# Linear-attention block: 1/std and softmax reciprocals by Ln and Exp on ScalarE, another order of the first loads, block diagonals on GpSimd

## The chip, the cores and the metric

The kernel runs on one core of a Trainium2 chip. A core has a matmul engine (TensorE, PE in the profile; its weight loads are PEld), a vector engine (VectorE, DVE), an activation engine (ScalarE, ACT), GpSimd (POOL) and SyncE (SP), which issues transfers. Each engine works through its own queue strictly in order and waits on semaphores of the others. Transfers are issued from the queues of SP and ACT. The metric is device microseconds (us) of one execution, median of several runs.

## The reference

One transformer block on x of 2048 rows by 640 columns, in bf16:

```python
h  = x + A(layernorm(x))          # linear attention, H = 32 heads of Dh = 20
h2 = h + B(layernorm(h))          # GeGLU, F = 1536
# A: q, k, v = x @ wqkv;  pq = q @ w_phi (per head), pk = k @ w_phi
phi_k = concat([softmax(pk), softmax(-pk)])      # phi_q likewise
kv = sum_s phi_k * v;  z = sum_s phi_k
o  = (phi_q @ kv) / (phi_q @ z + 1e-6);  A = o @ wo
# B: (gelu(x @ w_gate) * (x @ w_up)) @ w_down
# layernorm: (x - mean) / sqrt(var + 1e-5), no weights
```

## The kernel before

The 2048 rows are 16 tiles of 128 (t = 0 to 15), in four blocks b of four tiles. `NC` = 5 is the number of 128-row chunks of 640. The order of work is written out by hand (`manual_schedule`) for every engine: what a line issues goes to the end of its engine's queue. PSUM tiles for matmul results come from a rotating pool of four (three in the k loop) slots, `gtile`.

*Start (lines 160 to 384).* The first loads: x tile 0, tiles 2-3, W_v in three pieces, tiles 4-5, the transposed W_k (`WkT`) by a transposing DMA, tiles 8-11, `WqT`, tiles 12-15 on SP's queue; x tile 1, w_phi, tiles 6-7 on ACT's queue. Ten matmuls on zeros (`warm`) keep PE busy until x has come. For each of the first tiles: `ln_st` takes statistics on DVE (two `bn_stats` of 320 columns, one `bn_aggr`) and then 1/std on POOL (an add of eps and a `pow` of -0.5); `ln_ap` scales the tile on DVE (`ln_dve`); `ln_tp` transposes it on PE and copies it out of PSUM on ACT. `v_part` and `v_mm` are the v matmuls, `v_ev` their evacuation on ACT into one of six `vS` buffers (20 columns a head and a column of ones). w_phi is folded into W_k and W_q (`fold`): block diagonals `BD`, made on DVE at line 356 from w_phi and a mask, are multiplied with the transposed weights; the results are cast out of PSUM in turn by ACT and DVE.

*k loop (lines 388 to 421).* For each tile t: `k_tile` (k matmuls, and on ACT the exponentials E of +pk and -pk), `v_tile(t + 4)`, the layernorm of tile t+6 on ACT (`ln_act`, which also needs `mr`, the negated mean times 1/std, from POOL) and its transposing DMA, statistics of two later tiles, and `k_norm`: on DVE the sums over each head's 20 columns, 64 sums a tile (`sk`), and their reciprocals (`rs`); then v times the reciprocal (`vt`), the half of -pk on POOL and the half of +pk on DVE or POOL (`VP` lists the tiles for POOL; DVE's is put off to the next tile by `todo`). `kv_tile` multiplies E with vt into `kvp`, the sum over all tiles, four or five tiles later. At t = 15 four groups of q matmuls and their exponentials (`q_mm`, `q_exp`) are issued ahead of `k_norm(15)`; then come the k·v sums of tiles 10 to 15 and `kv_mask`.

*Attention and GeGLU (lines 610 to 665).* For each tile, stages `attn_a` (matmuls with kv), `attn_b`, `attn_b2`, `attn_b3` (the division, transposed by DMA), `attn_c` (matmuls with W_o, `po`), `attn_d`, `attn_d2` (residual sum, statistics, with a Square on ACT and small operations on POOL) and `attn_e` (layernorm on ACT, then a transposing DMA into the block's `LN2T`). `weave` puts them between units of matmul work: `gate_up` (one 128-row piece of gate and up for columns a0 to a1 of the block, then Gelu on ACT, product on DVE) and `down` (half the columns of one output tile). A stage with index i is issued ahead of unit i; stages with an index beyond the last unit are carried into the next weave, with the index counted from there:

```python
656  weave(gus(0, 0, 256) + downs(0, (0, 1)), ...)
659  weave(gus(0, 256, 512) + downs(0, (2, 3)), attn_at(7, 1, SHORT2))
SHORT2 = (0, 2, 3, 4, 10, 10, 11, 13)
```

The second weave has 12 gate units and 4 down units (0 to 15). The next one begins with `attn_a(8)` and the gate units of block 1, which read all four tiles of `LN2T`. Outputs are stored by SP a few units after their sums.

Of the kernel before, what the change touches and what calls it, by code (L numbers as in the profile page):

```python
# [17 lines left out]
def kernel(  # L18
# [16 lines left out]
    H = 32  # L35
# [11 lines left out]
    NWARM = 10  # L47
# [5 lines left out]
    WA, WB = 2,0  # L53
    T3 = 3
# [31 lines left out]
    nhalf = const.tile([P, 2], F32, name="nhalf")  # L86

# [11 lines left out]
    def ln_stats(pool, tiles, tag, act=True, between=None):  # L99
# [12 lines left out]
        nc.gpsimd.tensor_scalar_add(ve, mv[:, :, 1], EPS)  # L112
        rstd = small(pool, [P, n], "rstd" + tag)
        nc.gpsimd.tensor_tensor(rstd, ve, nhalf[:, 0:n], op=ALU.pow)  # L114
# [38 lines left out]
    vS = [p1.tile([P, H, VC], BF16, name=f"vS{i}") for i in range(6)]  # L153
# [6 lines left out]
    nc.gpsimd.memset(nhalf, -0.5)  # L160
    nc.sync.dma_start(x_sb[0][:, 0:1, :], x_v[:, 0:1, :])
    nc.scalar.dma_start(x_sb[0][:, 1:2, :], x_v[:, 1:2, :])
    nc.sync.dma_start(x_sb[0][:, 2:4, :], x_v[:, 2:4, :])
    for c0, c1 in ((0, 2), (2, 4), (4, 5)):
        nc.sync.dma_start(Wv[:, c0:c1, :], w_v[:, c0:c1, 2 * D:3 * D])

    ones = fp.tile([P, 2], F32, name="ones")
    nc.scalar.activation(ones, nhalf, ACTF.Exp)
    nc.scalar.dma_start(wphi, phi_v.rearrange("(c p) f -> p c f", p=P))
    nc.sync.dma_start(x_sb[1][:, 0:2, :], x_v[:, 4:6, :])  # L170
    nc.scalar.dma_start(x_sb[1][:, 2:4, :], x_v[:, 6:8, :])
    nc.sync.dma_start_transpose(WkT, A_wqkv[:, D:2 * D])
    wo_v = A_wo.rearrange("(c p) n -> p c n", p=P)
# [9 lines left out]
    for i in range(6):  # L183
        nc.vector.memset(vS[i][:, :, Dh], 1.0)
    make_identity(nc, ident)
    nc.gpsimd.memset(hmask, 1.0)
    for c in range(NC):
# [4 lines left out]
                                compare_op=ALU.is_ge, fill=0.0, base=Dh - 1 - off, channel_multiplier=-1)  # L192

# [36 lines left out]
    def ln_st(*tiles, act=True, between=None):  # L230
        for t, v in zip(tiles, ln_stats(p1, [x_sb[t // 4][:, t % 4, :] for t in tiles], "1", act, between)):
            lnp[t] = v
# [37 lines left out]
    def v_ev(t):  # L270
        nc.scalar.copy(vS[t % 6][:, :, 0:Dh].rearrange("p (u h) f -> p u h f", u=2),
                       pv[t][:, :, 0:HD].rearrange("p u (h f) -> p u h f", f=Dh))
# [5 lines left out]
    def k_tile(t):  # L278
# [3 lines left out]
        for s in range(2):  # L282
            nc.scalar.activation(Ek[t][:, s, :].rearrange("p (u f) -> p u f", u=2), pk[:, :, 0:HD],  # L283
                                 ACTF.Exp, scale=(1.0 if s == 0 else -1.0))

    def k_norm(t):


        sk = small(p1, [P, 2 * H], "sk")
        nc.vector.reduce_sum(sk, Ek[t].rearrange("p s (h f) -> p (s h) f", f=Dh), axis=AX.X)  # L290
        if t - 1 in todo:
            todo.pop(t - 1)()
        rs = small(p1, [P, 2 * H], "rs")
        nc.vector.reciprocal(rs, sk)  # L294
        Vt[t] = vt = ev.tile([P, 2, H, VC], BF16, name="vt", bufs=8)

        def mult(s, eng):
            eng.tensor_tensor(vt[:, s], vS[t % 6], rs[:, s * H:(s + 1) * H, None].to_broadcast([P, H, VC]), ALU.mult)  # L298

        mult(1, nc.gpsimd)  # L300
        if t in VP:
            mult(0, nc.gpsimd)
        elif t == NT - 1:
            mult(0, nc.vector)
        else:
            todo[t] = lambda: mult(0, nc.vector)

    todo = {}
# [36 lines left out]
    ln_st(0, act=False)  # L345
    ln_st(1, act=False)
    ln_ap(0, on_pe=True)
    ln_tp(0)
    warm(WA)
    ln_st(2, act=False, between=lambda: ln_ap(1, on_pe=True))  # L350
    ln_tp(1)
    warm(WB)
    ln_st(3, act=False)
    ln_ap(2, on_pe=True)

    nc.vector.tensor_tensor(BD, wphi[:, :, None, :].to_broadcast([P, NC, 8, Dh]),
# [340 lines left out]
```

The softmax here doesn't subtract the row's maximum and nothing guards it: scores larger than these inputs give would overflow.

## Time and profile before

| | |
|---|---|
| runs | 281.5, 281.89, 282.31 us; median 281.89 |
| the profiled execution | 281.18 us, of which the span from first to last instruction is 279.4 us |
| granted clock of TensorE | 1.00 |
| busy | PE 271.9, DVE 166.0, ACT 139.9, POOL 96.5 us |
| 1/std on POOL (line 114) | 8 of one column, mean 0.672 us; 5 of two columns, mean 0.713 us |
| reciprocals of k's sums (line 294) | 16, mean 0.547 us on DVE |
| k-loop layernorms on ACT (line 125) | 9, mean 0.933 us; on DVE (line 130) 9, mean 0.443 us |
| block diagonals (line 356) | 0.973 us on DVE |
| transposed W_k | issued at 4.52 us, 8.2 us from issue to landing |

How to read it: times in a chain or timeline are us from the start of the span, then the length. A chain is followed back from the last instruction to what released it at each step. "Idle before" is the time in which an engine had nothing running ahead of an instruction, and the arrow names what ended that. A busy PE includes its pipeline's latency, so neighbouring matmuls overlap in the timeline; the chain shows them end to end.

### The profile page before, as it was taken

What the parts mean: (1) busy time and instruction counts of PE and PEld (TensorE: products, weight loads), DVE (VectorE), ACT (ScalarE), POOL (GpSimd) and SP (SyncE); (2) the same over time, 40 slices, a digit from 0 to 9 for tenths busy, and PEclk for the clock granted to TensorE, in tenths of its full rate; (3) what the DMA queues carried; (4) which work ended last, traced back from release to release, by engine and by line L of the source; (5) the groups of instructions that cost most, each with busy time, mean ns of one, the idle gap of its engine ahead of it and who ended that gap; (6) DMA issues with size and microseconds to landing.
All of it is one profiled execution on the core that took longest, in us unless ns stands there. A gap on an engine that the chain in (4) does not pass through costs nothing.

```text
span 279.4 us, 5750 instructions
## 1 busy us (share of the span) xinstructions
PE 271.9 (97%) x2326; PEld 171.5 (61%) x2326; DVE 166.0 (59%) x289; ACT 139.9 (50%) x226; POOL 96.5 (35%) x211
## 2 busy tenths in 40 slices
PE   5899999999999999999999999999999999999995
PEld 2676677774655788788764555675455567444573
DVE  5899998789396586676324848322667532333222
ACT  2589888758596847355434454413446340222200
POOL 5448986794302216453401243300135230000000
PEclk9999999999999999999999999999999999999999
DMA  7991323694440021322520103221031513000011
GB/s 231 265 260 25 55 49 46 176 396 158 142 145 0 2 45 29 70 50 68 52 70 2 36 20 66 42 77 47 2 47 23 74 23 94 26 1 0 0 49 47
DMA packets 40347, 21.05 MB, mean 75 GB/s; under 512 B 33152, under 2 KB 38400, under 8 KB 40320
## 3 DMA queue, kind: packets, MB, share of 16 engines
q1 hardware_dynamic: 39376, 20.16, 28.8%
q10 hardware_dynamic: 944, 0.52, 0.7%
q8 instruction: 18, 0.29, 0.5%
q14 instruction: 9, 0.07, 0.1%
HBM read 10.18 MB, written 2.62 MB: 46 GB/s over the span
## 4 chain that ended last, share of the span: by engine, by line
PE 89%; DVE 4%; ACT 3%; DMA 1%; POOL 1%; issue 1%; ACTq 0%
PE gu L554 37%; PE pd L569 19%; PE pq L338 8%; PE po L509 8%; PE pk L251 7%; PE pv L251 5%; PE ab L449 2%; PE kvp L316 2%; DVE stats L106 1%; DMA x_sb<-in_A_x_dram 1%; DVE sk L290 1%; ACT E L283 1%; POOL rstd L114 1%; ACT Eq L343 1%; PE wa L215 1%
## 5 line engine op out<-in xcount | busy, mean ns | idle before, releaser
L557 ACT ACTIVATE g<-gu 128x512 bf16<-128x512 f32 (+1 forms) x60 | 30.7, 512 | 76.1 <-PE gu L554 75.1
L560 DVE TENSOR_TENSOR GT<-gu,g 128x512 bf16<-128x512 f32 (+1 forms) x60 | 34.5, 581 | 53.6 <-ACT g L557 53.4
L554 PE MATMUL gu<-LN2T,Wg 128*128 128x512 bf16 (+1 forms) x300 | 61.9, 337 | 0.5 <-DVE GT L560 0.4
L554 PE MATMUL gu<-LN2T,Wu 128*128 128x512 bf16 (+1 forms) x300 | 61.7, 336 | 0.0
L569 PE MATMUL pd<-Wd,GT 128*128 128x320 bf16 x384 | 53.8, 299 | 0.0
L569 PEld LDWEIGHTS <-GT 128*128 128x128 bf16 x384 | 37.4, 98 | 15.7 <-DVE GT L560 0.9
L554 PEld LDWEIGHTS <-Wu 128*128 128x128 bf16 x300 | 29.4, 98 | 22.6
L554 PEld LDWEIGHTS <-Wg 128*128 128x128 bf16 x300 | 28.4, 98 | 21.3 <-issue 0.5
L251 PEld LDWEIGHTS <-LN1T 128*128 128x128 bf16 x300 | 28.5, 98 | 11.6 <-issue 0.7
L298 POOL TENSOR_TENSOR vt<-vS,rs 128x672 bf16<-128x672 bf16 x22 | 29.2, 1345 | 9.1 <-DVE rs L294 8.5
L575 DVE TENSOR_TENSOR y<-pd,x_sb 128x640 bf16<-128x640 f32 (+1 forms) x17 | 13.3, 784 | 30.6 <-PE pd L569 30.6
L457 ACT COPY AB<-ab 128x704 f32<-128x704 f32 x28 | 19.5, 748 | 13.7 <-PE ab L449 13.5
L290 DVE TENSOR_REDUCE sk<-E 128x64 f32<-128x1280 bf16 x16 | 23.3, 1455 | 3.4 <-ACT E L283 3.4
L490 DVE TENSOR_TENSOR tt<-AB,w 128x1280 bf16<-128x1280 f32 x16 | 23.8, 1486 | 2.1 <-POOL w L483 2.0
L251 PE MATMUL pk<-Wk,LN1T 128*128 128x320 bf16 x160 | 24.1, 299 | 0.4 <-ACT E L283 0.3
L509 PE MATMUL po<-Wo,oT 128*128 128x320 bf16 x160 | 24.4, 299 | 0.0
L283 ACT ACTIVATE E<-pk 128x640 bf16<-128x640 f32 x32 | 20.8, 705 | 6.9 <-PE pk L251 6.7
L338 PE MATMUL pq<-LN1T,Wq 128*128 128x512 bf16 x100 | 22.9, 379 | 0.0
L251 PE MATMUL pv<-Wv,LN1T 128*128 128x320 bf16 x140 | 21.3, 299 | 0.0
L343 ACT ACTIVATE Eq<-pq 128x1024 bf16<-128x1024 f32 (+1 forms) x22 | 19.4, 950 | 3.7 <-PE pq L338 3.7
L509 PEld LDWEIGHTS <-oT 128*128 128x128 bf16 x160 | 15.6, 98 | 7.2 <-ACT oT L139 0.2
L125 ACT ACTIVATE ln<-x_sb,v,rstd 128x640 bf16<-128x640 bf16 x14 | 12.9, 919 | 10.5 <-POOL v L537 10.3
(80 smaller groups left out, 258.8 us busy)
## 6 DMA issues: line engine op xcount, KB each, us to landing
out_dram<-y SPq DMA_DIRECT2D x15, 160.0 KB, 1.8
Wg<-in_B_w_gate_dram SPq DMA_DIRECT2D x1, 1920.0 KB, 7.6
Wu<-in_B_w_up_dram SPq DMA_DIRECT2D x1, 1920.0 KB, 15.1
Wd<-in_B_w_down_dram SPq DMA_DIRECT2D x1, 1920.0 KB, 8.0
x_sb<-in_A_x_dram SPq DMA_DIRECT2D x2, 640.0 KB, 4.7
Wo<-in_A_wo_dram SPq DMA_DIRECT2D x1, 800.0 KB, 9.3
x_sb<-in_A_x_dram SPq DMA_DIRECT2D x2, 320.0 KB, 4.8
Wv<-in_A_wqkv_dram SPq DMA_DIRECT2D x2, 320.0 KB, 6.2
```

Of the source, the lines that this page charges most:

```text
L251: nc.tensor.matmul(ps[:, u, 0:HD], lhsT=lnT(t, c), rhs=W[:, c, u * HD:(u + 1) * HD], start=(c == 0), stop=(c == NC - 1))
L283: nc.scalar.activation(Ek[t][:, s, :].rearrange("p (u f) -> p u f", u=2), pk[:, :, 0:HD], ACTF.Exp, scale=(1.0 if s == 0 else -1.0))
L290: nc.vector.reduce_sum(sk, Ek[t].rearrange("p s (h f) -> p (s h) f", f=Dh), axis=AX.X)
L298: eng.tensor_tensor(vt[:, s], vS[t % 6], rs[:, s * H:(s + 1) * H, None].to_broadcast([P, H, VC]), ALU.mult)
L338: nc.tensor.matmul(pqs[j][:, i, :], lhsT=Wq2[:, kc, c * P:(c + 1) * P], rhs=LN1T[b][:, kc, :], start=(kc == 0), stop=(kc == NC - 1))
L343: nc.scalar.activation(Eq[j][:, :, s, :], pqs[j][:, 0:len(QG[j])], ACTF.Exp, scale=(1.0, -1.0)[s])
L490: nc.vector.tensor_tensor(tt.rearrange("p s (h f) -> p s h f", f=Dh), num, w[:, :, :, None].to_broadcast([P, 2, H, Dh]), ALU.mult)
L509: nc.tensor.matmul(po[:, u, 0:HD], lhsT=st[t][:, c, :], rhs=Wo[:, c, u * HD:(u + 1) * HD], start=(c == 0), stop=(c == NC - 1))
L554: nc.tensor.matmul(gu[:, i, 0:n], lhsT=W[:, c, f * P:(f + 1) * P], rhs=LN2T[b][:, c, a0:a1], start=(c == 0), stop=(c == NC - 1))
L557: nc.scalar.activation(g[:, 0:n], gu[:, 0, 0:n], ACTF.Gelu_apprx_tanh)
L560: nc.vector.tensor_tensor(st[b, "g", f][:, a0:a1], gu[:, 1, 0:n], g[:, 0:n], ALU.mult)
L569: nc.tensor.matmul(pd[:, u, 0:HD], lhsT=st[b, "g", f][:, tl * P:(tl + 1) * P], rhs=Wd[:, f, u * HD:(u + 1) * HD], start=(f == 0), stop=(f ...
```

## The change

- 1/std of tiles 0 to 3: `Ln(var + eps)` and `Exp(-0.5 ·)` on ACT (`log=True`) instead of POOL's add and pow; a table set that holds both functions is loaded at the top by hand.
- The reciprocals of k's sums: Ln and Exp on ACT (`k_rs`), for tile t-1 behind the exponentials of tile t; for tile 15 in `k_rs(15)` behind `k_norm(15)`. The sums are taken in two halves, and vt of tile t-1 follows the sums of tile t (`k_vt`).
- The layernorms of tiles 6 to 15 go from ACT (tile 6: DVE before too) to DVE, and POOL's `mr` with them.
- Block diagonals on POOL, right after the masks.
- Loads: x tile 1 on SP, tiles 2-3 on ACT ahead of w_phi, tiles 6-7 on SP behind the transposed W_k.
- The order of the first v matmuls, one warm-up matmul more at the top and one less later, 7 `vS` buffers, the pool's switch at tile 4 (`T3`) instead of 3.
- One Gelu on two columns ahead of the first real one; the last down unit in 192 and 128 columns; `attn_at(7, 3, SHORT2)` for `attn_at(7, 1, SHORT2)`.

```diff
-    NWARM = 10
+    NWARM = 11
-    WA, WB = 2,0
-    T3 = 3
+    WA = 1
+    T3 = 4
@@ ln_stats
-        nc.gpsimd.tensor_scalar_add(ve, mv[:, :, 1], EPS)
-        nc.gpsimd.tensor_tensor(rstd, ve, nhalf[:, 0:n], op=ALU.pow)
+        if log:
+            nc.scalar.activation(ve, mv[:, :, 1], ACTF.Ln, bias=eps)
+            nc.scalar.activation(rstd, ve, ACTF.Exp, scale=-0.5)
+        else:
+            nc.gpsimd.tensor_scalar_add(ve, mv[:, :, 1], EPS)
+            nc.gpsimd.tensor_tensor(rstd, ve, nhalf[:, 0:n], op=ALU.pow)
@@ loads
     nc.sync.dma_start(x_sb[0][:, 0:1, :], x_v[:, 0:1, :])
-    nc.scalar.dma_start(x_sb[0][:, 1:2, :], x_v[:, 1:2, :])
-    nc.sync.dma_start(x_sb[0][:, 2:4, :], x_v[:, 2:4, :])
-    for c0, c1 in ((0, 2), (2, 4), (4, 5)):
-        nc.sync.dma_start(Wv[:, c0:c1, :], w_v[:, c0:c1, 2 * D:3 * D])
-    ones = fp.tile([P, 2], F32, name="ones")
-    nc.scalar.activation(ones, nhalf, ACTF.Exp)
+    nc.sync.dma_start(x_sb[0][:, 1:2, :], x_v[:, 1:2, :])
+    nc.scalar.add_instruction(mybir.InstLoadActFuncSet(name=nc.get_next_instruction_name(), act_func_set_id=6))
+    nc.sync.dma_start(Wv[:, 0:2, :], w_v[:, 0:2, 2 * D:3 * D])
+    nc.scalar.dma_start(x_sb[0][:, 2:4, :], x_v[:, 2:4, :])
     nc.scalar.dma_start(wphi, phi_v.rearrange("(c p) f -> p c f", p=P))
+    nc.sync.dma_start(Wv[:, 2:4, :], w_v[:, 2:4, 2 * D:3 * D])
+    nc.sync.dma_start(Wv[:, 4:5, :], w_v[:, 4:5, 2 * D:3 * D])
     nc.sync.dma_start(x_sb[1][:, 0:2, :], x_v[:, 4:6, :])
-    nc.scalar.dma_start(x_sb[1][:, 2:4, :], x_v[:, 6:8, :])
     nc.sync.dma_start_transpose(WkT, A_wqkv[:, D:2 * D])
+    nc.sync.dma_start(x_sb[1][:, 2:4, :], x_v[:, 6:8, :])
@@ after the masks
+    nc.gpsimd.tensor_tensor(BD, wphi[:, :, None, :].to_broadcast([P, NC, 8, Dh]),
+                            hmask[:, :, :, None].to_broadcast([P, NC, 8, Dh]), ALU.mult)
@@ k_tile, behind the two exponentials
+        if t > 0:
+            k_rs(t - 1)
+    def k_rs(t):
+        sk = st1[t]
+        nc.scalar.activation(sk, sk, ACTF.Ln)
+        st1[t] = rs = small(p1, [P, 2 * H], "rs")
+        nc.scalar.activation(rs, sk, ACTF.Exp, scale=-1.0)
@@ k_norm
-        nc.vector.reduce_sum(sk, Ek[t].rearrange("p s (h f) -> p (s h) f", f=Dh), axis=AX.X)
-        if t - 1 in todo:
-            todo.pop(t - 1)()
-        rs = small(p1, [P, 2 * H], "rs")
-        nc.vector.reciprocal(rs, sk)
...
+        st1[t] = sk = small(p1, [P, 2 * H], "sk")
+        for s in range(2):
+            nc.vector.reduce_sum(sk[:, s * H:(s + 1) * H], Ek[t][:, s, :].rearrange("p (h f) -> p h f", f=Dh), axis=AX.X)
+    def k_vt(t):
+        rs = st1[t]
+        Vt[t] = vt = ev.tile([P, 2, H, VC], BF16, name="vt", bufs=8)
+        for s in (1, 0):
+            eng = nc.gpsimd if s == 1 or t in VP else nc.vector
+            eng.tensor_tensor(vt[:, s], vS[t % 7], rs[:, s * H:(s + 1) * H, None].to_broadcast([P, H, VC]), ALU.mult)
@@ start
-    ln_st(0, act=False)
-    ln_st(1, act=False)
-    ln_ap(0, on_pe=True)
+    ln_st(0, act=False, log=True)
+    ln_st(1, act=False, between=lambda: ln_ap(0, on_pe=True), log=True)
     ln_tp(0)
     warm(WA)
-    ln_st(2, act=False, between=lambda: ln_ap(1, on_pe=True))
+    v_part(0, 0, 1, 2)
+    ln_st(2, act=False, between=lambda: ln_ap(1, on_pe=True), log=True)
     ln_tp(1)
-    warm(WB)
-    ln_st(3, act=False)
-    ln_ap(2, on_pe=True)
-    nc.vector.tensor_tensor(BD, wphi[:, :, None, :].to_broadcast([P, NC, 8, Dh]),
-                            hmask[:, :, :, None].to_broadcast([P, NC, 8, Dh]), ALU.mult)
-    ln_ap(3, on_pe=True)
-    v_part(0, 0, 1, 2, 3, 4)
-    v_part(1, 0, 1)
-    ln_tp(2)
+    v_part(0, 3, 4)
+    v_part(1, 0, 1)
+    ln_st(3, act=False, between=lambda: ln_ap(2, on_pe=True), log=True)
+    ln_tp(2)
+    ln_ap(3, on_pe=True)
     v_part(1, 2, 3, 4)
     ln_tp(3)
@@ k loop
         if t > 0 and t + 6 < NT:
-            ln_ap(t + 6, on_act=True)
+            ln_ap(t + 6)
         if t % 2 == 0 and t + 8 < NT:
-            ln_st(t + 8, t + 9)
+            ln_st(t + 8, t + 9, act=False)
         k_norm(t)
+        if t > 0:
+            k_vt(t - 1)
+        if t == NT - 1:
+            k_rs(t)
+            k_vt(t)
@@ down, the last half tile
+        cuts = [(0, 192), (192, HD)] if last and u == 1 else [(0, HD)]
@@ behind q_exp(q + 6)
+    dummy = small(p2, [P, 2], "dummy", 1)
+    nc.scalar.activation(dummy, nhalf, ACTF.Gelu_apprx_tanh)
@@ second weave
-    weave(gus(0, 256, 512) + downs(0, (2, 3)), attn_at(7, 1, SHORT2))
+    weave(gus(0, 256, 512) + downs(0, (2, 3)), attn_at(7, 3, SHORT2))
```

## The prediction

> **What bounds the kernel now.** I read the page's busy shares first, then busy time by stretch, then the chain that ended last in order of time, then the timeline where the change touches something.
>
> ```profile
> PE 271.9 (97%) x2326; PEld 171.5 (61%) x2326; DVE 166.0 (59%) x289; ACT 139.9 (50%) x226; POOL 96.5 (35%) x211
> ```
> ```profile
> 0.00:16.86 16.86, 13.06 (x108) 8.21 (x109) 12.32 (x37) 7.98 (x13) 8.68 (x31) 1.00 0.98 256
> 16.86:31.61 14.75, 14.47 (x112) 10.28 (x111) 14.37 (x29) 12.47 (x20) 10.82 (x16) 1.00 0.36 90
> 31.61:72.49 40.88, 40.88 (x560) 28.36 (x560) 34.66 (x46) 32.55 (x47) 29.91 (x34) 1.00 0.49 146
> 144.14:276.46 132.32, 132.31 (x869) 73.28 (x868) 58.13 (x89) 45.10 (x76) 25.24 (x72) 1.00 0.16 36
> ```
> Columns: stretch, its length, busy us of PE, PEld, DVE, ACT, POOL, granted clock, DMA share, GB/s. From 31.61 on PE has work without a hole (but for 0.6 us near 95). So whatever makes DVE, ACT or POOL shorter there is worth nothing, and each wait that comes new to PE is paid in full. Something can be won only before 31.61, near 95 and behind the last matmul.
>
> ```profile
> 6.67 0.57 POOL rstd L114
> ...
> 9.74 1.42 POOL rstd L114
> ...
> 31.61 1.52 PE pk L251 x10
> ...
> 70.07 2.42 PE kvp L316 x120
> 72.49 2.27 PE pq L338 x10
> ...
> 134.67 1.36 PE po L509 x10
> 136.03 1.09 PE gu L554 x10
> 137.12 6.52 PE pd L569 x48
> 143.64 0.50 PE ab L449 x20
> 144.14 4.42 PE gu L554 x20
> ```
> Start, length, work. At the start the chain runs through POOL's 1/std; at 70 (the k·v sums) and at 144 (the second block's first gate matmuls) it is all PE. These two are where the change moves something to later:
>
> ```profile
> 69.03 2.92 ACT L343 ACTIVATE Eq<-pq 128x1024 bf16<-128x1024 f32 x4 [0.22 <-PE pq L338]
> 69.12 0.86 DVE L298 TENSOR_TENSOR vt<-vS,rs 128x672 bf16<-128x672 bf16 x1
> 69.19 1.97 POOL L298 TENSOR_TENSOR vt<-vS,rs 128x672 bf16<-128x672 bf16 x1 [1.34 <-DVE rs L294]
> ...
> 93.58 1.28 ACT L557 ACT_TABLE_LOAD   x1
> ```
> ```profile
> L298 POOL TENSOR_TENSOR vt<-vS,rs x22: 1309/1316/1969, 22.8 to 69.2; 128x672 bf16<-128x672 bf16 x22
> L298 DVE TENSOR_TENSOR vt<-vS,rs x10: 847/849/1009, 27.9 to 69.1; 128x672 bf16<-128x672 bf16 x10
> ```
> ```profile
> 137.44 0.73 ACT L530 ACTIVATE sq<-x_sb 128x640 bf16<-128x640 bf16 x1
> ...
> 139.75 0.92 ACT L125 ACTIVATE ln<-x_sb,v,rstd 128x640 bf16<-128x640 bf16 x1 [1.49 <-POOL v L537]
> ```
> ```profile
> DMA to landing us min/median/max: 2.5/2.6/4.5
> ```
> First fence: both halves of vt(15) are at work beside the last q exponentials, and end at 69.98 and 71.16, before PE needs them (72.09, see 3). The last two: tile 7's second layernorm, which lands (139.75+0.92+2.6) at 143.3, 0.9 us before the gate matmuls at 144.14.
>
> **The change, part by part.** Times are those of this execution's clock; who stands behind whom in a queue is read from the instruction order of the two built kernels.
>
> (1) *Start, to the fold of W_k (14.01 before).* Now: aggregate ends 5.09, POOL add and pow, scale at 6.10: 1.01 us. On ScalarE: Ln and Exp at 0.20 each (the 128x2 Exp at the top, 0.203) with 0.03 between: 0.5 us. So each scale could come 0.5 earlier, and the fourth, which waited for the 1.42 pow, 0.9. But the same engine copies the transposes out (0.69 each), in order: ahead of tile 0's copy now stands tile 1's Ln/Exp, which waits for tile 1's aggregate. Chain: statistics 3.96 to 5.09, Ln/Exp, scale 0 at 5.57; second half of tile 1's statistics and aggregate to 6.66; Ln/Exp to 7.11; copy 0 to 7.81, against 7.78 before. The gain is given back there. From copy 0 PE runs 6 v matmuls (0.82), transposes (0.28), 4 (0.54), waits for copy 1 to 9.86, 2 more weights of tile 1 (0.54), transposes, 0.82, 0.28, tile 2 (1.36) and half of 3 (0.68): fold at 13.82. Gain 0.2. Against it: x tiles 2-3 (320 KB) now go on ACT's queue beside tile 0 instead of behind it on SP's. Lower end 0, upper 0.9 (half of 4.8 less 3.1 us, the landings of 320 and 160 KB); I take 0.2, since SP's first packets lead. Tile 1 comes second on SP instead of first on ACT, near 4.5 instead of 4.1, and is wanted at 5.0: free. Sum of (1): 0, ends -0.4 (ACT's two at 0.15) and +0.7.
>
> What is nearly free here: block diagonals leave DVE (0.97) for POOL, (800/672)x1.345=1.6 us, ready by 8, needed at 14. The 11th warm-up matmul (0.43 at most) and the 7th buffer's memset (0.09) end before PE's first transposes and DVE's first x tile. The two-matmul warm-up becomes one, in time that PE waits anyway. There are two table loads before and after.
>
> But DVE and POOL get in each other's way: POOL's add took 0.41 beside the first scale (0.23 alone), and one DVE vt took 1.009 (0.849 alone) against a running POOL vt. So block diagonals that start ahead of a scale may hold it, by 0.16 (that row) or by their whole 1.6 us. At scale 1 this costs nothing: its transposes wait for PE's first 6 v matmuls until 8.66 anyway. At scale 0 it would count (rival A). The Trainium skill, SBUF — State Buffer, The single rule, speaks against the move more sharply than the rows: the two share one port pair, and whoever starts first holds it for its whole instruction. By that page a lost race costs the whole 1.6.
>
> W_k: its transposing DMA waits for x tile 0's landing (3.94) instead of tile 1's: issue 3.97, not 4.52; 6.11 us of issue on SP, to 10.1. Only then come x tiles 6-7 (before on ACT's queue at 1.72). They land 3.1 (160 KB) to 4.7 us (640 KB) later: 13.2 to 14.8; I take 13.4. DVE wants them at 13.0 (tiles 4 and 5's statistics, 4x0.41, behind scale 3); behind them stand DVE's W_k cast (14.6) and the scales of tiles 4 and 5, for which PE has about 0.4 us of slack, so 13.8 is early enough. Cost 0, upper end 1.0. x tiles 8-11 and W_q issue within 0.1 of before.
>
> Trainium skill, ScalarE: Activation LUTs, What ACT_TABLE_LOAD costs: an ACTIVATE with a per-partition bias is 0.28 us before its elements, not the row's 0.20; copy 0 would then come 0.3 later, and the sum below be 285.3.
>
> (2) *k loop, 16.9 to 62.5.* DVE: 16 reciprocals leave (8.8), 9 scales come (0.44 each, 4.0), the split sums cost some 0.1 more a tile (1.6): -3.2. POOL loses the small negated means (10 at 0.455). ACT: 9 scales leave (8.4), 32 Ln/Exp of 0.20+62x0.0008=0.25 come (8.2): even. The new wait: ACT's Ln of tile t-1 waits for DVE's sums; behind it queue v's evacuation and the next E. Adding DVE's rows in its new order (sums 1.5 a tile, a scale 0.4, a pair's statistics 1.9, vt 0.85, a W_q cast 0.75), sums 0 to 5 end near 21.8, 23.6, 27.2, 29.8, 33.4, 36.7, and ACT arrives after E of the next tile, near 22.5, 25.2, 28.0, 30.7, 33.7, 38.2: no wait. PE's holes of 0.08 at 26.7 (a transpose landing from ACT's late scale) and 0.28 at 31.3 (E of tile 4) close: -0.35; ends -0.4, +0.3.
>
> (3) *Last k tile.* Its Ln/Exp stand in ACT's queue behind the eight q exponentials, which end at 69.03+2.92=71.95, paced by PE's q matmuls. Then 2x0.25: 72.4. Both halves of vt(15) start there, DVE 0.86, POOL 1.97 as at 69.19, where the same two ran side by side: 73.3 and 74.4. PE has done tiles 10 to 14 at 70.07+100x0.0202=72.09 and has nothing else ahead of it; it ends the sums at 74.4+0.2=74.65 instead of 72.49. **+2.2**. Lower end with POOL's 1.32 alone: +1.5; upper 2.4. KV's masking shifts with it, covered by 2.27 of q as before.
>
> (4) *Dummy Gelu.* The table load already started 0.02 after the last Eq (93.58), with no wait in front; the dummy (0.20, less overlap) only stands ahead of the first g, which PE waits for near 95.4: +0.15; 0 to 0.2.
>
> (5) *Tile 7's start, 1 to 3.* Its attn_c goes from unit 11 to 13, its attn_e from 14 to 16, and the weave has units 0 to 15: it falls into the next one, though its order on PE shows one down unit (1.63) and one gate unit (1.09) now ahead of po: +2.72. po ends 138.75; statistics, square, POOL, ln and DMA took 7.2 from po's end (136.03) to 143.3, of which 0.5 was ACT busy with a g, absent now: landed 145.45. PE's next gate block needs all four tiles at 144.14: **+1.3**, ends 1.0 and 1.7. Cover: none, down units are done, attn_a(8) (0.50) is counted.
>
> (6) *Tail.* The last 320 columns split in 192 and 128: same matmul time; the last add is 0.29 instead of 0.49 (0.82 for 640, 0.49 for 320, so 1.03 ns a column): -0.2, ends -0.3, 0. The extra store issues (0.33) before the last one is ready.
>
> Sum: 0-0.35+2.2+0.15+1.3-0.2=+3.1. The profiled execution took 281.18, so 284.3; it lies 0.7 under the median 281.89, so **285.0**.
>
> **Rivals.** A: the block diagonals win the port before scale 0. w_phi landed 1.29+4.0=5.3 before, now behind 320 KB instead of 160: near 5.7, and scale 0 is due 5.6 to 5.8. For: a tie. Against: with scale 0 first, the block diagonals only meet scale 1. Price: scale 0 waits from 5.8 to 5.7+1.6-0.1=7.2, and the whole chain of (1) behind it, +1.4: 286.4. B: x tiles 6-7 late at 14.8: +1.0, 286.0. For: SP's 6.11 issue; against: 13.4 needs no help. C: one of the late stages is covered: without (3) 282.8, without (5) 283.7. For: an Eq run that ends earlier, or a quick landing; against: both orders are fixed. D, not slower: the four early 1/std really start PE 0.5 earlier and close all its holes up to 31.6 (0.46, 0.58, 0.31 and 0.36 beside its wait), 2.4 us at most; with the tail -0.2 and (3), (5) at their low ends (+2.5) that is 281.8. It decides from a gain of about 2.4 on; against it stands copy 0 at 7.81.
>
> **How the numbers follow.** Forecast 0.47 (own range 284.2 to 285.8), A 0.24, B 0.10, C 0.13, D 0.06. The range leaves out D and C's lower case, and takes in A with the upper ends of (3) and (5): 282.9 to 287.0. About 0.3% (0.85 us) is what a measurement can tell from no change. Faster 0.04 (most of D); same 0.05 (rest of D and C's lower case); slower 0.91.
>
> **What would show it.** PE idle of some 2 us between kvp matmuls, ended by POOL vt, just after the eighth Eq; PE idle of 1.3 before the first 512-wide gu, ended by DMA LN2T; fold of W_k within 0.4 of 14.0 (15.4 under A, with a first scale after 6.9); no wait of ACT on DVE sums. Wrong if kvp runs through, if LN2T lands before ab(8) ends, or if the k loop shows ACT waiting.

## The result and the profile after

The changed kernel took 292.96 us (median of 4 runs, 291.01 to 294.06) beside 281.83 us for the kernel before (281.50 to 282.31): 1.0386 times as long, 95% interval 1.0329 to 1.0443. The forecast of 285.0 us had the sign and missed the size; 292.96 lies outside its range of 282.9 to 287.0. The profiled execution took 293.0 us with a span of 291.3, against a span of 279.4 before: 11.9 us to be found.

The busy shares of the changed kernel, and its stretches from one event on TensorE to the next (columns as in the prediction):

```profile
PE 276.6 (95%) x2338; PEld 173.9 (60%) x2338; DVE 170.2 (58%) x299; ACT 140.4 (48%) x257; POOL 93.3 (32%) x195
```
```profile
0.00:16.47 16.47, 12.81 (x67) 6.94 (x68) 10.14 (x33) 6.97 (x16) 5.74 (x24) 0.90 0.99 255
19.32:68.71 49.39, 45.33 (x516) 33.15 (x515) 46.89 (x76) 34.59 (x73) 32.43 (x37) 1.00 0.41 121
68.71:81.29 12.58, 10.52 (x158) 5.91 (x156) 6.48 (x8) 9.34 (x17) 6.56 (x4) 1.00 0.14 55
81.29:102.94 21.65, 21.53 (x165) 11.03 (x166) 14.28 (x31) 14.46 (x18) 2.50 (x5) 0.92 0.28 92
156.13:288.57 132.44, 132.40 (x880) 73.83 (x880) 58.15 (x89) 43.74 (x75) 25.24 (x72) 1.00 0.17 37
```

The first row ends where the fold of W_k starts, the second runs from the first k matmul to the first q matmul, the third to the end of the products with vt, the fourth to the first gate and up matmul; the last is the second and following blocks, as long as before (132.32). From the fold to the first k matmul it is 2.85 us in both. The same events in the two traces:

| stretch | before, us | after, us | difference |
|---|---|---|---|
| start to fold of W_k | 14.01 | 16.47 | +2.46 |
| first k to first q matmul | 45.50 | 49.39 | +3.89 |
| first q matmul to end of products with vt | 10.13 | 12.58 | +2.45 |
| to first gate and up | 19.96 | 21.65 | +1.69 |
| rest (LN2T of tile 7, dummy Gelu, tail) | 186.98 | 188.36 | +1.38 |

These are TensorE's waits in the changed kernel: what it waited for, sum, number, longest. `tp` are the transposes and `pv` the v matmuls, whose waits on `ln` and `LN1T` (the first layernorm, and the same transposed) lie at the start, at 7.4 and 9.2 us; `wa` is the fold, here of W_q. All the others lie behind 31.6 us, where the kernel before had but one wait, of 0.4 us on GT.

```profile
PE pk L261 <- DVE Wq L236: 2.8, 2, 1.8
PE gu L566 <- DMA LN2T<-ln: 1.4, 1, 1.4
PE tp L144 <- DVE ln L136: 1.3, 1, 1.3
PE kvp L328 <- DVE vt L319: 1.3, 1, 1.3
...
PE pv L277 <- ACT LN1T L145: 1.1, 1, 1.1
PE wa L225 <- ACT Wq L234: 1.1, 1, 1.1
PE kvp L328 <- POOL vt L319: 0.8, 1, 0.8
```

The waits of kvp on vt and of gu on LN2T stand in the forecast, the one of tp on scale 0 in its rival A. The waits on W_q's evictions, in the middle of the k loop, stand nowhere in the prediction. The timeline of the changed kernel at the start shows rival A: the block diagonals begin 0.56 us ahead of scale 0, which then takes 1.15 us for 0.45.

```profile
5.65 1.53 POOL L201 TENSOR_TENSOR BD<-wphi,hmask 128x800 bf16<-128x800 bf16 x1 [2.01 <-DMA wphi<-in_A_w_phi_dram]
...
6.21 1.15 DVE L136 TENSOR_SCALAR ln<-x_sb,mv,rstd 128x640 bf16<-128x640 bf16 x1 [0.30 <-ACT rstd L117]
...
38.22 3.20 POOL L319 TENSOR_TENSOR vt<-vS,rs 128x672 bf16<-128x672 bf16 x2
...
38.48 1.77 DVE L319 TENSOR_TENSOR vt<-vS,rs 128x672 bf16<-128x672 bf16 x1
...
40.17 0.81 DVE L236 CAST Wq<-wa 128x640 bf16<-128x640 f32 x1
```

The last three lines are the k loop: both halves of a vt start together, VectorE's takes 1.77 us for 0.85, and the eviction of W_q for which TensorE waits stands behind it. And the clock, which in the trace of the kernel before never falls up to the last matmul, is halved twice (stretches of the changed kernel; the column after PE's busy time is the granted clock):

```profile
6.35:9.77 3.42, 1.24 (x11) 1.00 1.22 278
9.77:13.18 3.41, 3.41 (x20) 0.50 1.10 261
78.03:81.45 3.42, 1.36 (x46) 1.00 0.02 5
81.45:84.86 3.41, 3.41 (x10) 0.50 0.63 175
```

Each time a stretch of 3.41 us in which TensorE worked some 40% is followed by one at 0.5. In the second, ten q matmuls behind the wait for vt take 3.95 us; before they took 2.27.

```profile
78.87 2.00 POOL vt L319
...
81.29 3.95 PE pq L350 x10
```

That 1.68 is the table's fourth row, all but 0.01.

### The profile page after: what moved, and what is told of

It is laid out like the page before. It is cut to its first block, busy times and chain, and to the rows that moved or that the text cites. A ratio compares the mean times of both kernels' runs of the same rounds, so it can differ in the third digit from the quotient of the medians.

```text
span 291.3 us, 5793 instructions
## 1 busy us (share of the span) xinstructions
PE 276.6 (95%) x2338; PEld 173.9 (60%) x2338; DVE 170.2 (58%) x299; ACT 140.4 (48%) x257; POOL 93.3 (32%) x195
## 4 chain that ended last, share of the span: by engine, by line
PE 80%; DVE 9%; ACT 4%; DMA 2%; issue 2%; POOL 1%; DVEq 0%; ACTq 0%; POOLq 0%
PE gu L566 35%; PE pd L587 16%; PE po L521 7%; PE pq L350 6%; PE pk L261 5%; PE pv L261 4%; DVE sk L311 2%; PE ab L461 2%; ACT Eq L355 2%; DVE stats L107 2%; PE pv L277 1%; DVE ln L136 1%; DMA x_sb<-in_A_x_dram 1%; PE kvp L328 1%; DMA LN2T<-ln 1%
## 5 line engine op out<-in xcount | busy, mean ns | idle before, releaser
L587 PE MATMUL pd<-Wd,GT 128*128 128x320 bf16 (+2 forms) x396 | 54.0, 295 | 0.0
L587 PEld LDWEIGHTS <-GT 128*128 128x128 bf16 x396 | 38.0, 98 | 15.4 <-DVE GT L572 0.9
L319 POOL TENSOR_TENSOR vt<-vS,rs 128x672 bf16<-128x672 bf16 x22 | 32.5, 1499 | 12.9 <-ACT rs L303 12.8
L592 DVE TENSOR_TENSOR y<-pd,x_sb 128x640 bf16<-128x640 f32 (+3 forms) x18 | 13.5, 750 | 28.6 <-PE pd L587 28.6
L311 DVE TENSOR_REDUCE sk<-E 128x32 f32<-128x640 bf16 x32 | 24.4, 804 | 2.5 <-ACT E L293 2.4
L350 PE MATMUL pq<-LN1T,Wq 128*128 128x512 bf16 x100 | 24.6, 399 | 0.0
```

What stands on the lines that cost most here:

```text
L311: nc.vector.reduce_sum(sk[:, s * H:(s + 1) * H], Ek[t][:, s, :].rearrange("p (h f) -> p h f", f=Dh), axis=AX.X)
L319: eng.tensor_tensor(vt[:, s], vS[t % 7], rs[:, s * H:(s + 1) * H, None].to_broadcast([P, H, VC]), ALU.mult)
L350: nc.tensor.matmul(pqs[j][:, i, :], lhsT=Wq2[:, kc, c * P:(c + 1) * P], rhs=LN1T[b][:, kc, :], start=(kc == 0), stop=(kc == NC - 1))
L587: nc.tensor.matmul(pd[:, u, n0:n1], lhsT=st[b, "g", f][:, tl * P:(tl + 1) * P], rhs=Wd[:, f, u * HD + n0:u * HD + n1], start=(f == 0), sto ...
```

## The experiments

**One edit undone at a time.** Four kernels, each the changed one with one thing different. b and d put a part back; a puts back two, the scales on ScalarE and GpSimd's mr; c moves the last tile's sums and reciprocals further ahead than they were before.

```diff
@@ a_scale_act
-    ln_st(7, act=False)
+    ln_st(7)
-            ln_ap(t + 6)
+            ln_ap(t + 6, on_act=True)
-            ln_st(t + 8, t + 9, act=False)
+            ln_st(t + 8, t + 9)
@@ b_bd_vector
-    nc.gpsimd.tensor_tensor(BD, wphi[:, :, None, :].to_broadcast([P, NC, 8, Dh]),
...
     ln_tp(2)
+    nc.vector.tensor_tensor(BD, wphi[:, :, None, :].to_broadcast([P, NC, 8, Dh]),
...
     ln_ap(3, on_pe=True)
@@ c_last_early
             if t == QT[j]:
+                if j == 0:
+                    k_norm(t)
+                    k_vt(t - 1)
                 q_mm(j)
                 q_exp(j)
+                if j == 0:
+                    k_rs(t)
+                    k_vt(t)
...
-        k_norm(t)
-        if t > 0:
-            k_vt(t - 1)
-        if t == NT - 1:
-            k_rs(t)
-            k_vt(t)
+        if t < NT - 1:
+            k_norm(t)
+            if t > 0:
+                k_vt(t - 1)
@@ d_attn7_early
-    weave(gus(0, 256, 512) + downs(0, (2, 3)), attn_at(7, 3, SHORT2))
+    weave(gus(0, 256, 512) + downs(0, (2, 3)), attn_at(7, 1, SHORT2))
```

> The changed kernel with the scales of the k loop (x tiles 7 to 15) back on ScalarE; Ln and Exp of the k sums stay on ScalarE. Theory 'contention': in the changed kernel VectorE's scales and its half of vt run beside GpSimd's half of vt and are stretched by it (scales 0.70 to 1.43 us for 0.44, vt up to 1.79 us for 0.85), VectorE is full, and W_q's evictions and the sums come late. Then without the scales the stretch from the first k matmul to the first q matmul goes from 49.6 us back towards the 45.7 us of the kernel before, TensorE's waits of 2.8 us on VectorE's W_q evictions go, and the time is 288.5 to 290.0 us. Rival 'queue': ScalarE's Ln waits for VectorE's sums in front of the next exponentials, whoever scales. Then eight scales more on ScalarE (some 0.9 us each) make the loop no shorter: 49.6 us or more, 293 to 296 us.

> The changed kernel with the block diagonals back on VectorE, between the scales of x tiles 2 and 3. Theory 'block diagonals': GpSimd's product at 5.65 us stretches VectorE's scale of x tile 0 to 1.15 us (0.45 before), and TensorE's pauses that follow let its clock fall to 0.5 from 9.8 to 13.2 us. Then the scale takes 0.45 to 0.55 us, the clock stays at 1.0 in that window, the fold of W_k starts 1.5 to 2.4 us earlier, and the time is 290.6 to 291.6 us. Rival 'loads and logarithms': the start is late by x tile 0 landing 0.45 us later and by Ln and Exp on ScalarE behind the evictions. Then the product's time on VectorE (some 1.3 us) takes back what the scale gains, the clock still falls, and the time stays within 0.7 us of 293.

> The changed kernel with the sums of the last k tile ahead of everything that belongs to q, and its Ln and Exp behind the first two exponentials of q instead of behind all eight. Theory: the wait of TensorE for vt of tile 15 (1.27 and 0.79 us) goes; with it goes the fall of the clock to 0.5 from 81.4 to 84.9 us, which made ten q matmuls take 3.95 us for 2.27. From first q matmul to the end of the products with vt 12.4 us become some 10 (10.0 in the kernel before), and the time is 288.5 to 289.5 us. Rival 'clock apart': the clock falls whatever the wait, and the time is 290.3 to 291.0. Rival 'queue': the two small operations and the vt stand in other paths by then (exponentials of q later, TensorE waiting for them), and less than 1 us is gained: 292 to 293 us.

> The changed kernel with the attention of x tile 7 from place 1 of the last stretch of gate and up, as before, instead of 3. Theory: LN2T of tile 7 lands 1.4 us earlier and TensorE's wait of 1.4 us before the next gate and up goes: 291.3 to 291.9 us. Rival: the attention of tile 7 then meets that of tile 6 on VectorE and ScalarE, and TensorE waits for q, den or o instead: within 0.4 us of 293.

| kernel | median (range), us | ratio to before, 95% | stretch it was to mend |
|---|---|---|---|
| a_scale_act | 288.41 (288.22 to 290.89) | 1.0272, 1.0229 to 1.0314 | first k to first q: 46.41 |
| b_bd_vector | 290.07 (289.19 to 292.01) | 1.0332, 1.0286 to 1.0379 | fold of W_k at 14.44 |
| c_last_early | 288.56 (288.56 to 289.53) | 1.0265, 1.0247 to 1.0283 | q to end of products: 10.13 |
| d_attn7_early | 291.43 (289.48 to 293.15) | 1.0357, 1.0307 to 1.0406 | no wait for LN2T |

In the profiled executions each stretch was mended as its theory said, and no rival's stretch came: 2.98 us of the k loop's 3.89 (a), 2.03 of the start's 2.46 (b), all 2.45 of the last k tile (c), the 1.4 of LN2T (d). The times of b and d alone, with their intervals, don't stand clear of the changed kernel's 1.0329 to 1.0443. The times moved further than the stretches of a, b and c, those of a and b to below what was expected, and the clock is why: in c the wait for vt is gone, and in the profiled executions of a and b the clock did not fall behind that wait, though its 1.3 and 0.8 us were still there. In b it did not fall at the start either, but that was luck: two of b's four runs lost the clock once or twice (mean clock 0.994 and 0.988). d's profiled execution lost it for four stretches (0.977) and was its slowest. Scale 0 in b, with the path to itself (timeline):

```profile
6.13 0.45 DVE L136 TENSOR_SCALAR ln<-x_sb,mv,rstd 128x640 bf16<-128x640 bf16 x1 [0.30 <-ACT rstd L117]
```

**All four together, and the clock by itself.** The gains of the medians add up to 13.4 us, more than there was to lose.

e_all_four has the four diffs at once; g_more_warm has none of them, only more matmuls on zeros:

```diff
@@ g_more_warm
-    NWARM = 11
+    NWARM = 14
-    WA = 1
+    WA = 6
```

> The changed kernel with all four edits together: scales of the k loop on ScalarE, block diagonals on VectorE, sums and logarithm of the last k tile early, attention of tile 7 from place 1. Theory 'stages': each edit repairs its own stage, and what it gained beyond that was the clock, which can be lost once only. From the stages of the four runs: first k matmul at 17.3 us, 46.4 us to the first q matmul (45.5 in the kernel before), 10.1 us to the end of the products with vt, no wait for LN2T of tile 7; that is 1.3 us behind the kernel before at the end of the products, less 0.2 at the tail: 282.2 to 283.0 us. Rival 'sum': the four gains of the medians (4.6, 2.9, 4.4 and 1.5 us) add up, and the kernel is ahead of the one before: 279.5 to 280.3 us.

> The changed kernel with three more matmuls on zeros ahead of the first transpose and five more behind it, in TensorE's pauses of 1.3 and 1.1 us at the start; nothing else moves. Theory 'clock': a stretch in which TensorE does too little (0.36 busy from 6.35 to 9.77 us) brings the half clock of the next 3.41 us. Then the clock stays at 1.0, the fold of W_k starts at 14.8 to 15.2 us instead of 16.5, and the time is 291.3 to 291.8 us, or 289.6 to 290.1 where the later fall is missed too. Rival: the start hangs on VectorE's late scale and ScalarE's evictions, and TensorE's rate counts for nothing: fold at 16.2 to 16.7, 292.5 to 293.3 us.

e_all_four took 283.00 us (282.47 to 283.62; ratio 1.0055, 1.0038 to 1.0072): 'stages', at the upper end of its 282.2 to 283.0; the 279.5 to 280.3 of 'sum' fell. That the medians add up to too much is no proof of 'stages', though: by the ratios to before, the four gains are 1.1, 0.5, 1.2 and 0.3%, 3.2 together, and e gained 3.3. The stretches are the evidence: 46.59 us from first k to first q and 10.13 to the end of the products, close to the 46.4 and 10.1 expected; only the start was late (fold at 15.50, first k at 18.35 instead of 17.3), because the clock fell there in this execution, as in three of the six runs. What remains of the change costs 1.5 to 1.8 us.

g_more_warm took 289.98 (289.88 to 290.06; 1.0303, 1.0287 to 1.0319): 2.3 us by the ratios, 3.0 by the medians, gained by eight matmuls that compute nothing. The fold starts at 15.22 instead of 16.47, 0.02 above the upper end expected, and the clock is 1.00 throughout. The stretch that brought the half clock in the changed kernel, and the next, now read:

```profile
6.37:9.79 3.42, 2.92 (x19) 1.31 (x18) 3.11 (x8) 1.14 (x4) 0.81 (x1) 1.00 1.18 297
9.79:13.20 3.41, 3.17 (x33) 2.31 (x32) 2.53 (x8) 2.32 (x6) 0.00 (x0) 1.00 1.07 258
```

The wait for vt is untouched in g, and the clock did not fall there either: in this execution it lay across two stretches of 3.41 us, with 2.56 and 2.20 us of work.

```profile
74.64:78.05 3.41, 2.56 (x103) 2.04 (x102) 0.48 (x1) 2.81 (x6) 0.44 (x1) 1.00 0.02 5
78.05:81.47 3.42, 2.20 (x27) 1.22 (x27) 1.13 (x3) 0.51 (x1) 2.12 (x2) 1.00 0.13 10
```

**What slows the k loop.** a left open by which way the scales cost 3 us. First their order: VectorE's half of vt one tile later, as much work as before.

```diff
@@ f_vt_lag, k_vt (tile 15 and the tiles in VP as before)
...
+        else:
+            todo[t] = lambda: mult(0, nc.vector)
@@ f_vt_lag, loop over k tiles
             ln_ap(t + 6)
+        if t - 2 in todo:
+            todo.pop(t - 2)()
```

> The changed kernel with VectorE's half of vt one tile later than GpSimd's, so that it no longer starts with it; VectorE does as much work as in the changed kernel, its scales included. Theory 'contention': VectorE's vt takes 0.85 us again instead of up to 1.79, W_q's evictions come in time, and the stretch from first k to first q matmul falls from 49.4 to 46.5 to 48 us: 290 to 291.7 us. Rival 'load': VectorE is late because the scales are more work for it, however they lie; then the stretch stays at 49 to 49.6 us, and the time within 0.5 us of 293.

290.41 us (290.04 to 291.56; 1.0330, 1.0305 to 1.0355); first k to first q 48.23, just outside the 46.5 to 48 expected. The time fits 'contention', but its sign does not: VectorE's vt still took up to 1.97 us, now beside the next vt of GpSimd. 1.2 us went because W_q's eviction now stands ahead of vt and scale (38.52 instead of 40.17), and 1.7 because the clock did not fall at vt. It does not separate the two theories. A cleaner set followed. Its base, k_four_warm, is e_all_four with the two numbers of g; l_old_loads is that base with the loads' lines of the kernel before (the minus lines of the change's diff in place of its plus lines, the table load aside).

```diff
@@ i_dummy_scale, against k_four_warm
             ln_ap(t + 6, on_act=True)
+            xt, mean, rstd, mr = lnp[t + 6]
+            nc.vector.tensor_scalar(dum, xt, mean, rstd, op0=ALU.subtract, op1=ALU.mult)
@@ j_dummy_sum, against k_four_warm
             ln_ap(t + 6, on_act=True)
+            xt = lnp[t + 6][0]
+            nc.vector.reduce_sum(dum, xt[:, 0:340].rearrange("p (h f) -> p h f", f=Dh), axis=AX.X)
```

> The changed kernel with the four edits together and with the eight matmuls on zeros more at the start; the base of the three runs beside it. Theory 'clock': no half clock at the start, so the runs lie close together, 282.2 to 282.8 us; the fold of W_k starts at 14.3 to 14.7 us, and 46.4 to 46.6 us lie between first k and first q matmul. Rival: the matmuls on zeros delay real ones: fold at 15 us or later, 283 us or more.

> The base (four edits and more matmuls on zeros) with nine scales more on VectorE, in the place they have in the changed kernel, whose results nobody reads: the tiles themselves still come from ScalarE. ScalarE, GpSimd and TensorE do what they do in the base. Both theories, 'contention' and 'load': the stretch from first k to first q matmul grows from 46.5 to 48.3 to 49.5 us, with waits of TensorE on VectorE's W_q evictions; 284 to 285.7 us. A third, 'relief': what the scales cost in the changed kernel is that the tiles came late from VectorE. Then scales that nobody waits for cost nothing: 46.5 us, the time of the base.

> The base with nine sums over 340 elements in the same place, in place of the nine scales of the run beside it; results unread as well. A sum of 640 elements takes 0.81 us in the changed kernel with GpSimd's vt beside it or without, so one of 340 should take some 0.44 us, as long as a scale that has VectorE's path for itself. Theory 'contention': what counts is the stretching of the scales beside vt: 46.5 to 47.6 us from first k to first q, at least 1 us less than with the scales. Theory 'load': what counts is the work alone, 9 times 0.44 us: as long as with the scales, within 0.5 us.

> The base with the loads of x, W_v, w_phi and W_k issued in the order and on the queues of the kernel before. Theory: x tile 0 landed 0.45 us later in the changed kernel since its first loads share one queue; with the old order it lands at 3.9 us, all of the start moves up with it, and the fold of W_k starts 0.4 us earlier than in the base: 281.8 to 282.3 us. Rival: the start is bound by ScalarE's chain of logarithm, exponential and eviction, or by W_k landing later again: no change, within 0.2 us of the base.

| kernel | median (range), us | fold of W_k | first k to first q |
|---|---|---|---|
| k_four_warm | 283.31 (283.26 to 283.88) | 14.37 | 46.84 |
| i_dummy_scale | 284.06 (283.98 to 284.42) | 14.27 | 47.62 |
| j_dummy_sum | 283.51 (283.23 to 284.77) | 14.62 | 48.07 |
| l_old_loads | 283.31 (283.05 to 283.63) | 14.43 | 46.84 |

k: the four runs lie close together and the fold is where it was expected, but the time is 0.5 us above, in the rival's 283 or more, and no better than e: e's three runs without a fall of the clock took 282.47 to 282.76 us. Against e's profile, which had a fall, k gained 1.1 us at the start (fold at 15.50 there). Of this 0.25 was lost again in the loop, where a wait of 1.1 on ScalarE's v eviction stands in place of e's 0.6 on its layernorm, and 0.6 behind the first gate matmul, where TensorE waits 0.4 for a transposed `oT` that landed after 4.2 us instead of 2.6. i, j and l have that last wait too; why it landed late is open. These are k's waits between 17 and 66 us:

```profile
PE pk L258 <- ACT vS L278: 1.1, 1, 1.1
PE pv L258 <- DMA LN1T<-ln: 0.4, 1, 0.4
```

i: nine scales, at 0.43 to 1.25 us each, cost 0.78 us in the loop. Both theories had asked for 1.8 or more in the loop and fell on size; 'relief' fell too, at zero.

j: the profiled execution, at 284.77, is the odd one, with a transposing DMA that landed after 4.1 us instead of 2.6 and a wait of 1.2 on it; without that wait the stretch is 46.9, and the other three runs are at 283.23 to 283.52, 0.2 above k in the middle. So work that never lies in GpSimd's way (0.49 to 0.50 us each, whatever ran beside it) costs next to nothing, and work that does costs 0.8; neither costs 3.

l: the rival's time; x tile 0's scale started 0.58 us earlier (5.48), and the fold did not move. But this base could not show it: its 14 matmuls on zeros at the top still ran when scale 0 was done (5.93), and the transposes began behind them, at 6.85, against 6.56 in k. What the loads cost the changed kernel stays open.

In the k loop the changed kernel differs from i in two more things: the tiles come from VectorE's scales, with ScalarE relieved of them, and GpSimd no longer computes mr. In the tiles where statistics are made these products delayed GpSimd's vt, so that VectorE's ran first. mr can be given back alone (m), and the scales can be moved alone in the kernel before (o):

```diff
@@ m_warm_mr, against g_more_warm
-    ln_st(7, act=False)
+    ln_st(7)
-            ln_st(t + 8, t + 9, act=False)
+            ln_st(t + 8, t + 9)
@@ o_before_scales, against the kernel before
-            ln_ap(t + 6, on_act=True)
+            ln_ap(t + 6)
```

> The changed kernel with the eight matmuls on zeros more (289.98 us, 49.4 us from first k to first q matmul), and with GpSimd computing mr again for x tiles 7 to 15, which nobody reads: nine small products more (0.27 us each), the scales stay on VectorE. Theory 'pairing': in the tiles where the statistics are made, mr delays GpSimd's vt by some 0.6 us, VectorE's vt then runs ahead of it in 0.85 us for 1.77, and W_q's evictions come 0.9 us earlier each: the stretch falls to 47.4 to 48.2 us, 287.9 to 288.9 us, by more work for GpSimd alone. Rival 'scales': what VectorE is late by are the scales themselves, stretched wherever they lie; then the stretch stays at 49.2 to 49.8 us, 289.7 to 290.4 us.

> The kernel before with nothing but the scales of x tiles 7 to 15 on VectorE; GpSimd still computes mr, and the reciprocals stay on VectorE. Theory 'pairing': without vt starting on both engines at once the scales cost what the unread ones did, or less as ScalarE is relieved: 45.5 us from first k to first q matmul become 45.5 to 46.5, and the time is 281.2 to 282.3 us. Rival 'scales': VectorE full, W_q late, 2 us or more: 283.2 to 284.3 us.

m: 47.51 us from first k to first q, against 49.38 in g: nine small products more on GpSimd take 1.87 us out of the loop. 'Pairing' stands. Of g's two waits for W_q on VectorE, 2.8 us, the first all but goes (1.85 to 0.19); the second stays (0.98, now 1.10). g, then m:

```profile
PE pk L261 <- DVE Wq L236: 2.8, 2, 1.8
```
```profile
PE pk L261 <- DVE Wq L236: 1.3, 2, 1.1
```

The timeline of m:

```profile
35.98 1.10 POOL L125 TENSOR_SCALAR mr<-mv,rstd 128x1 f32<-128x1 f32 x2
36.10 0.85 DVE L319 TENSOR_TENSOR vt<-vS,rs 128x672 bf16<-128x672 bf16 x1
...
36.87 0.81 DVE L236 CAST Wq<-wa 128x640 bf16<-128x640 f32 x1
37.05 1.31 POOL L319 TENSOR_TENSOR vt<-vS,rs 128x672 bf16<-128x672 bf16 x1
```

VectorE's vt takes 0.85 us again, with GpSimd's behind it, and the cast for which TensorE waited follows at once. The median, 289.71 (288.32 to 290.06; 1.0275, 1.0244 to 1.0306), hides it: in the profiled execution the clock now fell behind the wait for vt, two more runs had its mean clock of 0.994, and the one with full clock took 288.32, inside the 287.9 to 288.9 expected. That is 1.7 us below g, which had it in every run.

o: 284.08 us (283.67 to 285.05; 1.0092, 1.0067 to 1.0116). Here my expectation fell and the rival's time came: scales alone cost 2 us or more in the kernel before, without the pairing (its vt took 0.85 us up to 60 us). In the profiled execution 48.08 us lie between first k and first q, 2.58 more than before; another 0.72 was lost at the start, which the edit does not touch. But the way is another than W_q; the waits of o from 17 to 67 us:

```profile
PE pv L251 <- DMA LN1T<-ln: 1.7, 2, 1.2
PE pv L251 <- ACT vS L271: 0.4, 1, 0.4
PE wa L215 <- ACT vS L271: 0.4, 1, 0.4
```

A wait of 1.2 is again on a slow landing, 4.4 us, of one transposing DMA; 0.5 is a scale that came late from VectorE. How much of o's 2.5 us is the scales and how much such landings or the start stays open.

**The tail, and a version ahead of both.**

h_before_tail is the kernel before with the change's new lines for the last down products, and nothing else; s_before_bd_later adds:

```diff
@@ s_before_bd_later, against h_before_tail
     ln_ap(2, on_pe=True)
+    ln_ap(3, on_pe=True)
     nc.vector.tensor_tensor(BD, wphi[:, :, None, :].to_broadcast([P, NC, 8, Dh]),
                             hmask[:, :, :, None].to_broadcast([P, NC, 8, Dh]), ALU.mult)
-    ln_ap(3, on_pe=True)
```

> The kernel before with nothing but the new tail: the last half tile's product in two pieces of 192 and 128 columns. Theory: the last VectorE add is shorter (0.29 us in the changed kernel) and the first store is under way earlier, 0.2 us less: 281.2 to 281.4 us beside 281.5. Rival: 10 more matmuls and one more store take the same time back: 281.5 to 281.8.

> The kernel before with its block diagonals on VectorE behind the scale of x tile 3 instead of ahead of it, and with the new tail. In the kernel before the product (0.97 us, from 9.75) holds GpSimd's power for tile 3 from 0.57 to 1.41 us, the scale of tile 3 starts at 11.18, and TensorE waits 0.43 us ahead of its transposes. Theory: the power takes 0.57 us, the scale starts at some 10.4, that wait goes, and the fold of W_k starts 0.4 us earlier, at 13.6; with 0.2 us of the tail 280.5 to 280.8 us beside 281.2. Rival: the product then delays the statistics of tiles 4 and 5 and the eviction of W_k, and the first k tile waits: 281.0 to 281.4 us.

h took 281.05 us beside 281.25 (ratio 0.9989, 0.9976 to 1.0002): 0.2 us as expected, and no more than the interval holds. s took 280.96 beside 281.54 (0.9982, 0.9966 to 0.9997): a version ahead of both kernels, if only by 0.2%, and not to be told from h. Its start did what was expected: the power for tile 3 and the product no longer meet (timeline of s),

```profile
9.73 0.56 POOL L114 TENSOR_TENSOR rstd<-ve,nhalf 128x1 f32<-128x1 f32 x1
...
10.32 0.45 DVE L130 TENSOR_SCALAR ln<-x_sb,mv,rstd 128x640 bf16<-128x640 bf16 x1 [0.50 <-POOL rstd L114]
10.68 0.98 DVE L357 TENSOR_TENSOR BD<-wphi,hmask 128x800 bf16<-128x800 bf16 x1
```

and the fold starts at 13.36, 0.42 us ahead of h's 13.78. But the first q matmul comes at 62.37, as in h (62.43): the k loop gives it back (46.17 us from first k to first q, 45.81 in h). Its waits, 0.3 for E and 0.3 for an LN1T, are little more than h's 0.3 and 0.2, so they show only part of how. In these two executions TensorE's holes at the start were not what set the end of the loop.

## Why the prediction was wrong, step by step

- **(1) start: 0 forecast, +2.46 measured.** The step itself went to rival A, which had 0.24, and A was too small at +1.4. From single profiled executions: 1.25 is the clock (16.47 to 15.22 in g), 0.78 the block diagonals on GpSimd (15.22 to 14.44 in b), 0.43 the rest, whose cause stays open; x tile 0's statistics began 0.45 later (4.41 for 3.96). A let scale 0 wait 1.4 us; held up, it took 0.70 longer. What A lacked was the clock that TensorE's pauses then cost, and the block diagonals are not needed for that: e has them on VectorE and lost the clock at the start too. Rival B did not happen: the statistics of tile 6 ran right behind those before them. ScalarE's Ln took 0.29 us at 128x1, not the row's 0.20; the figure of the Trainium skill weighed in (1) was the right one, and was worth 0.3 at most.
- **(2) k loop: -0.35 forecast, +3.89 measured. This is the step that failed.** It added VectorE's rows as they are alone, "a scale 0.4, a pair's statistics 1.9, vt 0.85", and booked the products mr as work saved: "POOL loses the small negated means". Durations for two engines that hold each other up can't be added that way: in the changed kernel a scale took up to 1.43 us and VectorE's vt up to 1.79. The prediction had this mechanism in (1), for the block diagonals, and did not carry it into the loop, where vt runs on GpSimd 22 times. The runs divide it, each by one profiled execution: 0.9 with the scales back on ScalarE, so for Ln, Exp and the rest of the rearrangement (46.41 in a, against 45.50); 1.1 for the scales on VectorE with mr kept (47.51 in m, against a; unread scales cost 0.8); 1.9 for the loss of mr, by which both vt start together (49.38 in g, against m). The last is one edit and clear. The border between the first two is not: a lacks m's eight matmuls on zeros, and against k, which has them (46.84), the shares are 1.3 and 0.7. The forecast "no wait of ACT on DVE sums" fell too: ScalarE's Ln waited twice, for 1.6 and 0.7 us. (In the sum for ScalarE, 32 times 0.25 is 8.0, not 8.2; nothing hangs on it.)
- **(3) last k tile: +2.2 forecast, +2.45 measured**, by the mechanism named. What the prediction missed is what such a wait does to the clock: +1.68 more in the profiled execution, and not in every one.
- **(4)** +0.15 forecast; TensorE's wait for GT behind the table load grew from 0.4 to 0.5. **(5)** +1.3 forecast, 1.4 measured, and gone in d. **(6)** -0.2 forecast, -0.2 in h, no more than that run's interval.

Added up, the steps that hang on the order of one queue, (3) to (6), came within 0.3 us each. Most of the 8.8 us beyond the forecast is two things. One is VectorE and GpSimd holding each other up, which the old trace shows in single rows only, as a power of 1.42 us for 0.57 and a vt of 1.01 for 0.85: 0.8 at the start, 1.9 by the pairing in the loop, and part of the 0.7 to 1.1 that the scales cost there. How much of that part is plain work is not shown. The other is the clock (1.25 and 1.68). The rest is 0.4 at the start, some 0.9 of the loop, the 0.35 that was forecast to gain there, and 0.25 in (3).

## What to carry to other kernels

Before work goes from one engine to another, list what GpSimd and VectorE will then run at the same moment, and price a scale or a VectorE operation with two inputs in SBUF that starts beside a running GpSimd vt up to the end of that vt, and 0.2 us (a scale) or 0.7 us (a vt) beyond, as the timelines here have it; small work that is taken off GpSimd can make things worse, if it kept the two apart. A pause of TensorE has a price beyond its length: where a stretch of 3.41 us falls under about half work, count 1.3 to 1.7 us more, as here, or fill the pause with matmuls on zeros. And a gain is worth only what the next wait leaves of it: 0.4 us at the start of s were returned in the k loop, and of k's 1.1 some 0.8 came back as waits further on.

## What the runs showed of the hardware

**The clock goes by fixed stretches, and its threshold is near 46%.** In all traces where the granted clock falls and rises it does so on a grid of 3.413 us, whose phase differs from run to run. By the trace, in which the ends of matmuls are modelled, stretches in which TensorE was busy 1.00 to 1.55 us were followed by 0.50, those of 1.57 us and more at full clock by 1.00; at 1.56 both occurred (d and b):

```profile
38.81:42.22 3.41, 1.56 (x46) 1.19 (x45) 3.41 (x5) 1.20 (x4) 3.41 (x3) 1.00 0.01 2
42.22:45.63 3.41, 3.41 (x19) 2.12 (x18) 3.41 (x8) 0.92 (x2) 1.53 (x2) 0.50 0.25 49
```
```profile
36.49:39.90 3.41, 1.56 (x43) 1.30 (x37) 3.41 (x5) 1.10 (x3) 3.41 (x3) 1.00 0.01 2
39.90:43.31 3.41, 3.41 (x31) 2.54 (x30) 3.41 (x10) 2.72 (x6) 0.86 (x2) 1.00 0.46 91
```

So whether a wait of 2 us costs 1.7 more depends on where it falls on the grid. It goes with the spread: the four runs of the changed kernel, 291.01, 292.92, 293.00 and 294.06 us, had mean clocks of 0.994, 0.988, 0.988 and 0.982, while g, with full clock, stayed within 0.2 us. The Trainium skill, TensorE: Matmul & The Clock Gate, Part 1, has the free-running window of 3413 ns, which agrees; but its rule of thumb under HAM oscillation, no idle gaps beyond some 3.4 us, is too mild here, where pauses of 1.3 and 0.8 us in one window were enough.

**Who waits for whom.** The Trainium skill, SBUF — State Buffer, The single rule, names VectorE operations with two inputs in SBUF as contending with GpSimd's reads, scales as able to contend with it, and sums on Trainium2 as never doing so. The runs agree: scales 0.43 us alone and up to 1.43 beside vt, vt 0.84 alone and up to 2.01, while the changed kernel's sums on VectorE stayed at 0.76 to 0.82 us whatever ran beside them. It holds in the other direction too: in the kernel before, GpSimd's power took 1.42 us beside VectorE's block diagonals, and 0.56 in s without them.
